# Attention's scores and row-max scores as pairs of matmuls in 64-column halves of TensorE

## The chip, the cores and the metric

The kernel runs on one core of a Trainium2 chip. Its time is the device time of one execution in microseconds (us), the median over several runs; the less the better. The engines are TensorE (PE in the rows; PEld is its weight load), VectorE (DVE), ScalarE (ACT), GpSimd (POOL) and SyncE (SP, which issues most DMAs). TensorE multiplies a stationary operand, the weights, of up to 128 rows (the contraction) and 128 columns (the partitions of the result) by a moving operand that is streamed through it, and writes to PSUM. Shapes in the rows are written 128\*64 (rows and columns of the weights) and 128x288 (partitions and streamed columns of the moving operand).

## What is computed

Three blocks follow each other. Attention over 4 batches of 8 heads, 1152 positions of 64 values, with the queries pooled by twos; then a router that sends each of 2304 tokens of 512 values to one of 8 experts; then a dense feed-forward block.

```python
def _attn_ref(q, k, v):
    B, H, S, D = q.shape                       # 4, 8, 1152, 64
    q_pool = q.reshape(B, H, S // 2, 2, D).mean(axis=3)
    scores = scale * np.matmul(q_pool, k.transpose(0, 1, 3, 2))
    scores = scores - np.max(scores, axis=-1, keepdims=True)
    attn = np.exp(scores)
    attn = attn / (np.sum(attn, axis=-1, keepdims=True) + 1e-09)
    return np.matmul(attn, v)
...
    logits = x @ w_gate + modality_bias[modality_id]      # router
    out[mask] = gate_w[mask, None] * (np.maximum(x[mask] @ w1[e], 0.0) @ w2[e])
...
    g = softplus(x @ w_in)                                # dense block
    return g @ w_out
```

## The kernel before

Attention is worked off by pairs of heads, 16 of them (`p`). For each pair there are float16 operands whose 128 rows hold the 64 values of a head twice: `KA` is the rounded key, in both halves; `Q[:,:,0]` holds the rounded query in one half and what the rounding left over in the other; `KB` and `Q[:,:,1]` hold the rest of the key against the rounded query, and in rows of the other half the row maximum that is subtracted. Every product of these contracts over all 128 rows.

Three steps on TensorE take nearly all of attention's time there:

- `srow` (L117, and L120 for the tile that holds 64 queries of each head): row-max scores of 128 queries against 384 keys into the tile `sr` (three buffers), 27 such rows a pair of heads. VectorE reduces each to its maximum (`mx`, L121). `mfin` turns the maxima of a pair into rows of `Q` (L140, L144).
- `smat` (L168, L169): the scores of 128 keys against 288 queries for both heads into `st` (two buffers), four matmuls; `ex` (L172, ScalarE) makes the exponentials `P` of them (five buffers). A pair of heads has 18 such groups (`g`), nine for each half of the queries.
- `pv` (L212): values times `P` in float32, the two heads in the two column halves of the array, 64 columns each, into `pv`.

Beside these, `add` (L186, POOL, L184 on DVE for one pair) sums `P` over three groups into `acc`, `rsum` (L197, L202) sums over partitions in 32-column matmuls, and after each batch of four pairs `lstage` does the router's steps for its tokens: sums and transposes (L227, L238, L285), ranks (L296 to L298), and a chain of small steps on VectorE.

The order is written by hand. For each group the main loop issues the scores of the next group, then its exponentials, then row-max rows (about 1.5 a group, some 27 groups ahead of need, by the formula in `rows`) between single steps of other work (casts of the next heads, loads, `rsum`, router steps), then `pv` for two groups at once at odd chunks and for one at the ninth, then `add`. Each engine works off its instructions in that order. On TensorE a group so reads: four scores in 128 columns, one or two row-max rows in 128 columns, and in about every second group four or eight pv matmuls in 64 columns.

After the 288th group come the router's last steps, the experts' blocks and the dense block; all their matmuls use float16 high and low parts.

Of the kernel before, what the change touches and what calls it, by code (L numbers as in the profile page):

```python
# [16 lines left out]
def attention(ctx,late,tc,I,C,x_dram,LG,gate,fill,early):  # L17

    nc=tc.nc
# [89 lines left out]
    def srow(r):  # L109
        p,w=divmod(r,SRN); t,kh=divmod(w,3)  # L110
        ka,q=KA[p%NS],Q[p%NS]
        if w==0: MX[p]=smp.tile([128,9,3],F32,name="mx")
        sr=srp.tile([128,512],F32,name="sr")
        h,r0=TILES[t]
        k0=kh*KW
        if h<2:
            nc.tensor.matmul(sr[:,:KW],lhsT=q[:,h,0,r0:r0+128],rhs=ka[:,h,k0:k0+KW],start=True,stop=True)  # L117
        else:
            for hh in range(2):
                nc.tensor.matmul(sr[64*hh:64*hh+64,:KW],lhsT=q[:,hh,0,r0:r0+64],rhs=ka[:,hh,k0:k0+KW],start=True,stop=True)  # L120
        nc.vector.tensor_reduce(out=MX[p][:,t,kh:kh+1],in_=sr[:,:KW],axis=AX.X,op=ALU.max,negate=True)  # L121

    def mfin(p,ta=0,tb=9):
# [36 lines left out]
    def dec(g):  # L160
        p,s=divmod(g,18); half,c=divmod(s,9)
        return p,half,c
    def smat(g):
        p,half,c=dec(g); ka,kb,q=KA[p%NS],KB[p%NS],Q[p%NS]
        st=stp.tile([128,2,512],F32,name="st"); ST[g]=st
        qs=slice(half*HQ,half*HQ+HQ); ks=slice(c*128,c*128+128)
        for h in range(2):
            nc.tensor.matmul(st[:,h,:HQ],lhsT=ka[:,h,ks],rhs=q[:,h,0,qs],start=True,stop=False)  # L168
            nc.tensor.matmul(st[:,h,:HQ],lhsT=kb[:,h,ks],rhs=q[:,h,1,qs],start=False,stop=True)  # L169
    def ex(g):  # L170
        P[g]=pp.tile([128,2,HQ],F32,name="P")
        nc.scalar.activation(out=P[g],in_=ST.pop(g)[:,:,:HQ],func=ACTF.Exp,scale=1.0/16)  # L172
# [235 lines left out]
    while done<6: srow(done); done+=1  # L408
    C['cl1'](); C['setup']()
    while done<15: srow(done); done+=1  # L410
# [4 lines left out]
    while done<R0: srow(done); done+=1  # L415
    for f in MF[1:]: f()
    smat(0); ex(0)
    ones()
    for g,f in C['later']: at(g,f)
# [7 lines left out]
    for g in range(NG+1):  # L427
        if g+1<NG: smat(g+1)
        if g>=1 and g-1<NG:
            p,half,c=dec(g-1)  # L430
            if c==NCH-1: evac(p,half)
        if g+1<NG: ex(g+1)
        tgt=rows(g)
        es=ev.pop(g,[])
        while pend and pend[0][0]<=g: pend.pop(0)[1]()
        while done<tgt-(g<18) or es:
            if done<tgt-(g<18): row(g)
            if es: es.pop(0)()

        if g<NG:  # L440
            c=dec(g)[2]
            for k in ((g-1,g) if c%2 else (g,) if c==NCH-1 else ()): pv(k)
        while done<tgt: row(g)
        if g<NG: add(g)
# [607 lines left out]
```

## Time and profile before

| | us |
|---|---|
| median of 3 runs | 1153.48 |
| lowest, highest of them | 1151.69, 1153.79 |
| profiled execution | 1149.53 |
| its span, first to last instruction | 1147.7 |
| attention's exponentials, first to last (L172) | 22.8 to 504 |

The profile is of one execution. Its rows give, for a group of instructions, line, engine, operation, the tile written and those read, the shapes and the count, then busy time and the mean duration in ns, then the time that the engine was idle just before. A matmul's duration goes from its start to the modelled end of its result, and following matmuls overlap; how fast TensorE works is therefore read from the starts. In a list in order of time, rows with a count hold several instructions of one kind, and their duration goes from the first start to the last end.

### The profile page before, as it was taken

The numbers are of one execution on the slowest core, as the hardware profiler recorded it, in microseconds if no ns is written. First come the engines' busy times: TensorE is split into PE (matmuls) and PEld (weight loads), VectorE is DVE, ScalarE is ACT, GpSimd is POOL, SyncE is SP. The second block draws the span as 40 slices with busy tenths as digits, with TensorE's granted clock in tenths as the row PEclk, the third lists the DMA queues.
The fourth block names the chain that finished last, engine by engine and source line by source line (L and its number), as shares of the span: only waits on it lengthen the run. The fifth ranks groups of instructions, "written<-read, shape, count | busy, mean of one in ns | idle before, by whom it ended". The sixth has DMA issues, their size and how long they took to land. (4 is left out here: it accounts for less than half of the span.)

```text
span 1147.7 us, 20868 instructions
## 1 busy us (share of the span) xinstructions
PE 1082.5 (94%) x7887; PEld 641.0 (56%) x7887; DVE 865.6 (75%) x1583; ACT 641.2 (56%) x1096; POOL 504.9 (44%) x532
## 2 busy tenths in 40 slices
PE   5998999999999999998989898999999999999996
PEld 2444555455555554566877777885444444446662
DVE  5778798768877787969789888739967767676762
ACT  5666656675666655556556556647444444444441
POOL 7888877888688867644423233110000100100101
PEclk9999999999999999999999999999999999999999
DMA  9334427441654041335677787731100000000000
GB/s 250 79 84 111 120 64 197 113 120 38 182 149 113 24 130 53 116 127 193 211 261 253 277 279 271 265 125 46 37 10 28 28 10 19 37 1 11 37 10 31
DMA packets 42940, 129.48 MB, mean 113 GB/s; under 512 B 5841, under 2 KB 12881, under 8 KB 40914
## 3 DMA queue, kind: packets, MB, share of 16 engines
q1 hardware_dynamic: 39794, 118.12, 34.2%
q0 software_dynamic: 3040, 9.96, 2.5%
q8 instruction: 65, 1.06, 0.4%
q14 instruction: 41, 0.34, 0.1%
HBM read 108.13 MB, written 20.45 MB: 112 GB/s over the span
## 5 line engine op out<-in xcount | busy, mean ns | idle before, releaser
L121 DVE TENSOR_REDUCE mx<-sr 128x1 f32<-128x384 f32 x432 | 225.4, 550 | 92.8 <-PE sr L117 73.9
L172 ACT ACTIVATE P<-st 128x576 f32<-128x576 f32 x288 | 186.0, 651 | 154.0 <-PE st L169 142.5
L186 POOL TENSOR_TENSOR acc<-P 128x288 f32<-128x288 f32 x192 | 160.6, 858 | 84.0 <-ACT P L172 80.3
L796 POOL DMA_INDIRECT out_dram<-io,CIDS x18 | 21.1, 1174 | 359.1 <-ACT io L794 312.7
L212 PE MATMUL pv<-P,v 128*64 128x288 f32 x1152 | 174.5, 419 | 0.3 <-ACT P L172 0.3
L168 PE MATMUL st<-Q,KA 128*128 128x288 f16 x576 | 155.4, 291 | 0.0
L169 PE MATMUL st<-Q,KB 128*128 128x288 f16 x576 | 153.6, 288 | 1.8 <-ACT Q L152 1.8
L186 POOL TENSOR_TENSOR acc<-acc,P 128x288 f32<-128x288 f32 x176 | 148.5, 864 | 9.0 <-ACT P L172 7.3
L117 PE MATMUL sr<-KA,Q 128*128 128x384 f16 x384 | 113.6, 335 | 17.2 <-DVE mx L121 8.7
L611 PE MATMUL l<-xf,WIH 128*128 128x256 f16 (+1 forms) x384 | 125.1, 326 | 1.0 <-ACT xf L817 1.0
L612 PE MATMUL l<-xf,WIH 128*128 128x256 f16 (+1 forms) x384 | 125.1, 326 | 0.2 <-DVE xf L818 0.2
L613 PE MATMUL l<-xf,wl 128*128 128x256 f16 (+1 forms) x384 | 125.1, 326 | 0.0
L648 ACT ACTIVATE mhl<-mraw 128x512 f16<-128x512 f32 x160 | 98.1, 625 | 45.3 <-DMA mraw<-in_wm_dram 22.2
L653 DVE SCALAR_TENSOR_TENSOR mhl<-mraw,mhl 128x512 f16<-128x512 f32 x140 | 95.7, 703 | 27.3 <-ACT mhl L648 26.5
L212 PEld LDWEIGHTS pv<-P,v 128*64 128x64 f32 x1152 | 70.4, 136 | 72.9 <-issue 35.6
L787 PE MATMUL o<-WOH,g 128*128 128x512 f16 x288 | 109.1, 379 | 1.2 <-ACT io L794 0.8
L788 PE MATMUL o<-wl,g 128*128 128x512 f16 x288 | 109.1, 379 | 0.0
L789 PE MATMUL o<-WOH,g 128*128 128x512 f16 x288 | 109.1, 379 | 0.0
L168 PEld LDWEIGHTS <-KA 128*128 128x128 f16 x576 | 56.3, 98 | 85.5 <-issue 75.4
L770 ACT ACTIVATE e<-e 128x1024 f32<-128x1024 f32 x36 | 38.0, 1057 | 101.3 <-DVE m L768 101.3
L94 POOL TENSOR_TENSOR KB<-kr,KA 64x576 f16<-64x576 f32 x64 | 83.3, 1305 | 4.3 <-ACT KA L90 2.1
L612 PE MATMUL l<-hT,mhl 128*128 128x256 f16 x288 | 78.5, 272 | 6.4 <-DVE hT L680 6.4
(246 smaller groups left out, 2162.0 us busy)
## 6 DMA issues: line engine op xcount, KB each, us to landing
mraw<-in_wm_dram SPq DMA_DIRECT2D x80, 512.0 KB
kr<-in_k_dram SPq DMA_DIRECT2D x30, 576.0 KB
qr<-in_q_dram SPq DMA_DIRECT2D x16, 576.0 KB
v<-in_v_dram SPq DMA_DIRECT2D x16, 576.0 KB
mraw<-in_w_out_dram SPq DMA_DIRECT2D x16, 512.0 KB
stg<-in_w_in_dram SPq DMA_DIRECT2D x12, 512.0 KB
y_dram<-w SPq DMA_DIRECT2D x20, 256.0 KB
xs_dram<-xs SPq DMA_DIRECT2D x24, 192.0 KB
```

Of the source, the lines that this page charges most:

```text
L117: nc.tensor.matmul(sr[:,:KW],lhsT=q[:,h,0,r0:r0+128],rhs=ka[:,h,k0:k0+KW],start=True,stop=True)
L121: nc.vector.tensor_reduce(out=MX[p][:,t,kh:kh+1],in_=sr[:,:KW],axis=AX.X,op=ALU.max,negate=True)
L168: nc.tensor.matmul(st[:,h,:HQ],lhsT=ka[:,h,ks],rhs=q[:,h,0,qs],start=True,stop=False)
L169: nc.tensor.matmul(st[:,h,:HQ],lhsT=kb[:,h,ks],rhs=q[:,h,1,qs],start=False,stop=True)
L172: nc.scalar.activation(out=P[g],in_=ST.pop(g)[:,:,:HQ],func=ACTF.Exp,scale=1.0/16)
L186: for h in range(2): nc.gpsimd.tensor_tensor(out=A[:,h],in0=B_[:,h],in1=P[g][:,h],op=ALU.add)
L212: nc.tensor.matmul(t[64*h:64*h+64,:HQ],lhsT=V[p][:,c,64*h:64*h+64],rhs=P[g][:,h],start=(c==0),stop=(c==NCH-1))
L611: nc.tensor.matmul(o,lhsT=wh_,rhs=x[0],start=first,stop=False)
L612: nc.tensor.matmul(o,lhsT=wh_,rhs=x[1],start=False,stop=False)
L613: nc.tensor.matmul(o,lhsT=wl_,rhs=x[0],start=False,stop=last)
L787: nc.tensor.matmul(o,lhsT=g[:,0,i,cs],rhs=WOH[:,fc],start=(fc==0),stop=False)
L788: nc.tensor.matmul(o,lhsT=g[:,0,i,cs],rhs=WOL(fc),start=False,stop=False)
```

## The change

Each matmul of the scores, 128 columns wide, becomes two of 64 columns: the first 64 keys into partitions 0 to 63 of `st`, the other 64 into partitions 64 to 127, with the same moving operand. Each row-max matmul of 128 columns becomes two of 64 queries in the same way, as those of L120 were already. The operands, their types and the sums are the same.

```diff
@@ srow
-        if h<2:
-            nc.tensor.matmul(sr[:,:KW],lhsT=q[:,h,0,r0:r0+128],rhs=ka[:,h,k0:k0+KW],start=True,stop=True)
-        else:
-            for hh in range(2):
-                nc.tensor.matmul(sr[64*hh:64*hh+64,:KW],lhsT=q[:,hh,0,r0:r0+64],rhs=ka[:,hh,k0:k0+KW],start=True,stop=True)
+        for i in range(2):
+            hh,r=(h,r0+64*i) if h<2 else (i,r0)
+            nc.tensor.matmul(sr[64*i:64*i+64,:KW],lhsT=q[:,hh,0,r:r+64],rhs=ka[:,hh,k0:k0+KW],start=True,stop=True)
@@ smat
-        qs=slice(half*HQ,half*HQ+HQ); ks=slice(c*128,c*128+128)
+        qs=slice(half*HQ,half*HQ+HQ)
         for h in range(2):
-            nc.tensor.matmul(st[:,h,:HQ],lhsT=ka[:,h,ks],rhs=q[:,h,0,qs],start=True,stop=False)
-            nc.tensor.matmul(st[:,h,:HQ],lhsT=kb[:,h,ks],rhs=q[:,h,1,qs],start=False,stop=True)
+            for i,w in enumerate((ka,kb)):
+                for o in (0,64):
+                    nc.tensor.matmul(st[o:o+64,h,:HQ],lhsT=w[:,h,c*128+o:c*128+o+64],rhs=q[:,h,i,qs],start=(i==0),stop=(i==1))
```

In the changed file the row-max matmuls stand in L118, the scores in L168, pv in L211, the transposes in L284 and the exponentials in L171. Two places show what it does to the order on TensorE. The first is the seam between row maxima, pv and the next scores; a row gives line, operation, result and operands, and the size of the result (the float32 matmuls of L212 load their weights themselves). Before:

```order
L169 LDWEIGHTS KB_194
L169 MATMUL st<-Q_197,KB_194 128x288
L117 LDWEIGHTS Q_196
L117 MATMUL sr<-KA_190,Q_196 128x384
L212 MATMUL pv<-P,v 64x288 x4
L168 LDWEIGHTS KA_191
L168 MATMUL st<-Q_197,KA_191 128x288
```

The same place now:

```order
L168 LDWEIGHTS KB_194
L168 MATMUL st<-Q_197,KB_194 64x288
L118 LDWEIGHTS Q_196
L118 MATMUL sr<-KA_190,Q_196 64x384
L118 LDWEIGHTS Q_196
L118 MATMUL sr<-KA_190,Q_196 64x384
L211 MATMUL pv<-P,v 64x288 x4
L168 LDWEIGHTS KA_191
L168 MATMUL st<-Q_197,KA_191 64x288
L168 LDWEIGHTS KA_191
L168 MATMUL st<-Q_197,KA_191 64x288
```

Where results of 128, 64 and 128 partitions followed each other, all have 64 now; nothing changes its place.

The second is a transpose of the router's stage (L285, `xu` against an identity, 96 columns, which are over 64). Before:

```order
L117 LDWEIGHTS Q_195
L117 MATMUL sr<-KA_189,Q_195 128x384
L285 MATMUL sr<-ident,xu 96x128 x4
L168 LDWEIGHTS KA_191
L168 MATMUL st<-Q_197,KA_191 128x288
```

And now:

```order
L118 LDWEIGHTS Q_195
L118 MATMUL sr<-KA_189,Q_195 64x384
L118 LDWEIGHTS Q_195
L118 MATMUL sr<-KA_189,Q_195 64x384
L284 MATMUL sr<-ident,xu 96x128 x4
L168 LDWEIGHTS KA_191
L168 MATMUL st<-Q_197,KA_191 64x288
```

Here the transposes, which stood among wide matmuls, stand between 64-column ones. Counted over the whole program, steps between the wide and the 64-column form are 358 before and 74 now, steps to or from 32-column matmuls 110 in both.

## Rows read from the trace of the kernel before

**Rows 1.** The page, part 1: engine, busy us, share of span, instructions.

```profile
PE 1082.5 (94%) x7887; PEld 641.0 (56%) x7887; DVE 865.6 (75%) x1583; ACT 641.2 (56%) x1096; POOL 504.9 (44%) x532
```

**Rows 2.** Four stretches: length, busy us (instructions) by engine, granted clock, DMA.

```profile
core 0: us, PE busy (x) PEld busy (x) DVE busy (x) ACT busy (x) POOL busy (x), PEclk, DMA share, GB/s
181.56:301.86 120.30, 117.48 (x946) 61.40 (x944) 93.95 (x206) 78.05 (x142) 99.36 (x113) 1.00 0.44 118
211.09:224.56 13.47, 13.47 (x105) 7.05 (x103) 11.73 (x19) 10.50 (x19) 11.91 (x13) 1.00 0.78 215
239.74:253.21 13.47, 13.47 (x105) 7.05 (x103) 11.04 (x21) 10.51 (x19) 12.72 (x13) 1.00 0.86 242
268.44:284.87 16.43, 15.34 (x131) 8.29 (x131) 16.09 (x41) 10.98 (x22) 14.74 (x16) 1.00 0.17 53
```

**Rows 3.** Waits from 60 to 490 us: total us, times, longest us.

```profile
ACT P L172 <- PE st L169: 125.5, 137, 3.6
POOL acc L186 <- ACT P L172: 80.6, 66, 3.1
...
DVE mx L121 <- PE sr L117: 60.9, 77, 2.1
...
ACT P L172 <- POOL acc L186: 8.7, 18, 1.1
...
PE sr L117 <- DVE mx L121: 6.4, 7, 2.1
```

**Rows 4.** Groups of TensorE's instructions by line and shape, the whole span.

```profile
L212 PE MATMUL pv<-P,v 128*64 128x288 f32 x1152 | 174.5, 419 | 0.3 <-ACT P L172 0.3
L168 PE MATMUL st<-Q,KA 128*128 128x288 f16 x576 | 155.4, 291 | 0.0
L169 PE MATMUL st<-Q,KB 128*128 128x288 f16 x576 | 153.6, 288 | 1.8 <-ACT Q L152 1.8
L117 PE MATMUL sr<-KA,Q 128*128 128x384 f16 x384 | 113.6, 335 | 17.2 <-DVE mx L121 8.7 <-ACT KA L90 8.2
...
L120 PE MATMUL sr<-KA,Q 128*64 128x384 f16 x96 | 16.8, 356 | 2.7 <-DVE Q L86 1.4 <-DVE mx L121 0.8
```

**Rows 5.** TensorE's matmuls in order of time, 300 to 304 us: start, duration.

```profile
300.03 1.14 PE L212 MATMUL pv<-P,v 128*64 128x288 f32 x8
301.10 0.30 PE L168 MATMUL st<-Q,KA 128*128 128x288 f16 x1
...
301.48 0.29 PE L169 MATMUL st<-Q,KB 128*128 128x288 f16 x1
301.69 0.35 PE L120 MATMUL sr<-KA,Q 128*64 128x384 f16 x2
301.98 0.64 PE L285 MATMUL sr<-ident,xu 128*96 128x128 f32 x4
302.45 0.33 PE L117 MATMUL sr<-KA,Q 128*128 128x384 f16 x1
302.71 0.71 PE L212 MATMUL pv<-P,v 128*64 128x288 f32 x4
303.35 0.30 PE L168 MATMUL st<-Q,KA 128*128 128x288 f16 x1
...
303.85 0.33 PE L117 MATMUL sr<-KA,Q 128*128 128x384 f16 x1
304.01 0.38 PE L285 MATMUL sr<-ident,xu 128*96 128x128 f32 x2
```

**Rows 6.** Matmuls and weight loads in order of time, 58.5 to 59.4 us.

```profile
58.75 0.14 PEld L120 LDWEIGHTS <-Q 128*64 128x64 f16 x4 [0.24 <-issue]
58.75 0.52 PE L120 MATMUL sr<-KA,Q 128*64 128x384 f16 x4
...
58.94 0.55 PEld L212 LDWEIGHTS pv<-P,v 128*64 128x64 f32 x6
...
59.10 0.65 PE L212 MATMUL pv<-P,v 128*64 128x288 f32 x4
```

## The prediction, made before the changed kernel was run

> **What bounds the kernel now.** I read the busy times of the page first, then the stretches of the attention loop, then who waits for whom, and last the starts of single matmuls. TensorE (PE) is busy for 94% of the span, VectorE (DVE) for 75%, GpSimd (POOL) for 44% [rows 1]. The change touches only attention, so its stretches count. Four pairs of heads (72 groups) repeat there every 120.30 us, at a granted clock of 1.00; in that period PE is busy 117.5 us, POOL 99.4, DVE 94.0 and ACT 78.1 [rows 2]. The list of waits has the same direction everywhere: from 60 to 490 us the exponentials on ACT wait 125.5 us for the score matmuls, POOL 80.6 us for the exponentials, the row maxima on DVE 60.9 us for the row-max matmuls, while the row-max matmuls wait only 6.4 us for a buffer that DVE frees, and ACT 8.7 us for a buffer that POOL frees [rows 3]. PE sets the pace; DVE and POOL are each some 80% loaded and wait for it.
>
> Busy PE is not PE at its peak, so the starts of the matmuls have to be read. Wide matmuls of 288 columns follow each other every 0.125 us: the four scores from 303.35 take until the L117 at 303.85 [rows 5]. The pv matmuls (L212) run as pairs in two column halves. Two pairs last 0.65 us where nothing is in their way (59.10, [rows 6]), four last 1.14 (300.03, [rows 5]): 0.49 us for two more, so a pair every 0.245 us, and 0.405 us from a matmul's start to its end. Now the seams. The last of the four pairs starts at 300.76 (300.03 and three times 0.245) and the next wide matmul at 301.10, 0.34 us instead of 0.245: **leaving the 64-column form costs 0.10 us.** From the wide L117 at 302.45 to L212 it is 0.26 us; from the same kind of L117 at 303.85 to the wide L285 it is 0.16: 0.10 us on entering. Then the two pairs from 302.71 last 0.71 instead of 0.65 us: another 0.05 to 0.06, because its weights were not loaded ahead. **Entering pv costs 0.15 us.** From L169 at 301.48 to the row-max pair L120 it is 0.21 instead of 0.125, 0.09, and such a first pair takes 0.19 us until the next one (58.75 to 58.94) where the second takes 0.16 (58.94 to 59.10) [rows 6]: together 0.11. It is not the change of type: L117 (float16) to L285 (float32) at 303.85 shows no loss, and neither does L120 (float16) to L212 (float32) from 58.94 to 59.10 [rows 5, 6].
>
> **The change, part by part.** It takes no arithmetic out. Each of 1152 wide score matmuls (L168 and as many of L169) becomes a pair, and so do the 384 wide row-max matmuls; the 96 narrow row-max matmuls and the 1152 of pv are narrow already [rows 4]. PE gets 1536 more matmuls and as many more weight loads; the order of the work is the same on every engine but for a few rows on ACT near 500 us, which I cost at nothing: a copy and an exponential trade places while ACT waits for PE.
>
> What goes are seams. In the order of the instructions 329 steps between the wide and the 64-column form go: 127 into pv, 33 into narrow row-max pairs, 169 back into wide matmuls. New are 45, around what stays wide (transposes, ranks, the early expert blocks). Those that lead to 32-column matmuls stay, with another neighbour. The sum of PE time: 127 x 0.15 = 19.0, 33 x 0.11 = 3.6, 169 x 0.10 = 16.9, together 39.5 us; a new seam at 0.12 us (301.69 to 301.98, from a row-max pair to a transpose, is 0.29 where 0.16 would do [rows 5]; with what DVE's waits at the rank matmuls hide I leave it there), 45 x 0.12 = 5.4 us. **Net 34 us on PE, 284 seams of 0.12 us.**
>
> What the pairs themselves cost is not in the trace for scores: no float16 pair of 288 columns runs there. The near rows bound it. From below: a pv pair of 288 float32 columns takes 0.245 us, just twice the 0.125 of one wide float16 matmul, and the second row-max pair at 58.94 takes 0.16 us, as a wide one does; so a pair that has its weights takes as long as the wide matmul, and no gain is possible in it, the columns being streamed as before. From above: the first pair after a seam takes 0.03 us more, with its loads uncovered. The loads are covered where the pairs follow each other: four loads of two row-max pairs are done in 0.14 us, and the loads of pv start at 58.94, in the moment in which the last row-max pair starts [rows 6]. I take nothing for it; at 0.03 us the 1536 pairs would take back 46 us.
>
> The Trainium skill has a rule against this: "TensorEngine Tiling (Array Packing)", section Restrictions and Gotchas, says that column tiling excludes the Fast Weight Load, and "TensorE: Matmul & The Clock Gate", Part 3, that a load overlaps matmuls in flight only where the row groups differ or where it goes to the background weight buffer. All pairs here use all 128 rows. The loads at 58.94 run beside matmuls on the same rows, so the trace speaks for the second half of that sentence; by its first half alone the third rival below would be the forecast.
>
> **How much of the 34 us arrives.** PE is the pace, but not by far. The period of 120.30 us has 82 seams less and 12 more: 70 x 0.12 = 8.4 us, so 111.9, in which POOL's 99.4 us would be 89% and DVE's 94.0 84% [rows 2]. Stretch by stretch it is tighter. The nine groups from 211.09 lose 10 seams, 13.47 to 12.27 us, with DVE busy 11.73: it fits, barely, and I take 1.0 of 1.2. Those from 239.74 also lose 10, but POOL has 12.72 us of work there: at most 0.75, I take 0.7. Those from 268.44, with the router's steps on DVE, lose a net 3, 16.43 to 16.07, and DVE has 16.09: I take 0.2 of 0.36 [rows 2]. So 1.9 of 2.76 in these three, the tightest of their kinds, and nearly all elsewhere: about three quarters. Queues smooth it: five P buffers let POOL lag some four groups, three sr buffers let DVE lag three row maxima. What is late next is then POOL's acc for the P buffers (the wait of 8.7 us grows) and DVE's mx for the sr buffers (the 6.4 us). Of the 34 us, 30 seams (3.6 us) lie before 60 us, where loading and DVE hold PE too: half. The other 30.5 at three quarters are 23: **25 us in all.** After attention nothing is changed, and what is there starts after its end, so that the gain is carried to the end. The profiled execution took 1149.53 us: 1124.5. The median of the three runs is 4 us above it, 1153.48: **1128.5 us.**
>
> **Rivals.**
> 1. DVE and POOL take the pace over, because they need their slack within three to six groups and not nine: the stretches from 239.74 and 268.44 are then the rule. Against it: both wait for PE for most of their idle time [rows 3]. Gain 10 to 19 us, say 14.5: 1139.
> 2. Everything arrives, since a DVE or POOL burst in one stretch is made good in the next: 34 us, 1119.5. For it: utilisation in the period stays under 90%.
> 3. **Slower:** the weight loads of float16 pairs are not covered. One mechanism, at every pair of the scores, where only 0.125 us lie between one pair's start and the next, in which two loads have to end; it decides from 34/1536 = 22 ns a pair on. At 0.03 to 0.05 us (the first pairs after a seam, [rows 5, 6]) it costs 46 to 77 us: some 1153.5-34+60 = 1180. Against it: the loads at 58.75, four in 0.14 us [rows 6].
> 4. The change does not do what it says: the 0.10 us belong to pv's end and not to the form, and stay in front of the narrow scores. For it: no row shows a narrow float16 matmul behind pv. Against it: the same 0.09 to 0.10 us stand on entering, in front of L120 as in front of L212. The entering half alone goes then, 22.6 of the 39.5 us, less 5.4 for the new seams 17, of which some 10 arrive past DVE and POOL: 1143; if neither half goes, 1153.
>
> **How the numbers follow.** Forecast 0.60 (own range 1121 to 1134), rival 1 0.19, rival 2 0.09, rival 3 0.06, rival 4 0.06, half of it at no change. The range takes in the forecast, rival 2 and nearly all of rival 1: 1118 to 1141. A measurement of this kernel tells about 0.2% (2.3 us) from no change. Faster by more: 0.60+0.19+0.09+0.03 = 0.91; same 0.03; slower 0.06.
>
> **What would show it.** Right: a score pair starts 0.24 us after the last pv pair, not 0.34; score pairs follow each other every 0.125 us, with their loads starting beside the pair before; the period of 120.3 us falls to 112 to 115 us; DVE and POOL keep their busy time and their share rises; after attention all is alike but earlier. Wrong: score pairs every 0.15 us or more (rival 3), 0.34 us still behind pv (rival 4), or the seams gone and the matmuls waiting for mx or P in their place (rival 1).

## The result, and the profile after

| | before | after |
|---|---|---|
| median of 9 runs each, us | 1152.55 | 1139.08 |
| lowest, highest, us | 1147.16, 1154.40 | 1133.89, 1145.03 |
| profiled execution, its span, us | 1149.53, 1147.7 | 1137.12, 1135.3 |
| attention's exponentials, first to last, us | 22.8 to 503.6 | 22.7 to 488.0 |

The ratio is 0.9884, with an interval of 0.9864 to 0.9904: 13.5 us faster. The forecast of 25 us was right in its sign and about twice the size; the time lies where the first rival put it, 1139.

The page's first part, after; engine, busy us, share, instructions [rows 1]:

```profile
PE 1058.7 (93%) x9423; PEld 707.6 (62%) x9423; DVE 870.0 (77%) x1583; ACT 640.8 (56%) x1096; POOL 502.3 (44%) x532
```

PE has 1536 more matmuls and is busy 23.8 us less. But its idle time, span less busy, rose from 65.2 to 76.6 us. DVE and POOL kept their busy time, within 4.4 and 2.6 us, as expected.

In attention alone, from the first exponential to the last, PE's busy time fell by 27.0 us, though two stretches at half clock there (below) lengthen it by up to 3.4. First the kernel before, then the changed one:

```profile
core 0: us, PE busy (x) PEld busy (x) DVE busy (x) ACT busy (x) POOL busy (x), PEclk, DMA share, GB/s
22.80:503.60 480.80, 463.52 (x3696) 241.46 (x3695) 380.08 (x808) 305.27 (x554) 385.16 (x431) 1.00 0.40 109
22.70:488.00 465.30, 436.49 (x5213) 306.48 (x5210) 384.08 (x804) 305.75 (x555) 382.17 (x431) 0.99 0.41 113
```

The seam of [rows 5] in the timeline of PE, after (start, duration):

```profile
290.23 1.14 PE L211 MATMUL pv<-P,v 128*64 128x288 f32 x8
291.20 0.29 PE L168 MATMUL st<-Q,KA 128*64 128x288 f16 x2
291.32 0.29 PE L168 MATMUL st<-Q,KB 128*64 128x288 f16 x2
291.44 0.29 PE L168 MATMUL st<-Q,KA 128*64 128x288 f16 x2
291.56 0.29 PE L168 MATMUL st<-Q,KB 128*64 128x288 f16 x2
291.69 0.33 PE L118 MATMUL sr<-KA,Q 128*64 128x384 f16 x2
```

The last of the four pv pairs starts at 290.23 and three times 0.245, 290.965; the first score pair comes 0.235 us later, where it was 0.34. From there a pair starts every 0.12 us, as fast as one wide matmul did. The weight loads are hidden; a load and a matmul pair a little earlier:

```profile
288.65 0.29 PE L168 MATMUL st<-Q,KA 128*64 128x288 f16 x2
288.65 0.12 PEld L168 LDWEIGHTS <-KB 128*64 128x64 f16 x2
```

While the `KA` pair of 288.65 streams, the two `KB` loads of the pair that follows at 288.78 take 0.12 us: they just fit. A new seam, from a row-max pair to a transpose, costs 0.10 us over the 0.16 between two row-max pairs:

```profile
292.34 0.33 PE L118 MATMUL sr<-KA,Q 128*64 128x384 f16 x2
...
292.60 0.31 PE L284 MATMUL sr<-ident,xu 128*96 128x128 f32 x1
```

So the prices read at single places hold. What differs is what became of the sum, stretch by stretch. The table has the time of 18 groups (one pair of heads, from its first exponential to the next pair's), and the gain on PE worked out with the prediction's prices from the seams in the order of that pair, all in us; the sixteen pairs' gains add up to 34.0.

| pair of heads | seams' worth | before | after | gained |
|---|---|---|---|---|
| 5 (as 9) | 2.44 | 29.53 | 27.18 | 2.35 |
| 6 (as 10) | 2.60 | 28.65 | 26.77 | 1.88 |
| 7 (as 11) | 2.24 | 28.70 | 27.14 | 1.56 |
| 1 | 2.56 | 30.43 | 32.20 | -1.77 |
| 4, with router steps | 1.16 | 33.44 | 33.09 | 0.35 |
| 8, with router steps | 1.16 | 33.42 | 36.22 | -2.80 |
| 12, with router steps | 1.16 | 33.41 | 34.01 | -0.60 |
| 13 | 2.03 | 31.60 | 31.11 | 0.49 |
| all 16, from the first to the last exponential | 34.0 | 480.8 | 465.3 | 15.5 |

The plain pairs of the middle got 70 to 96% of their worth. The three router pairs together lost 3.0 us where the seams were worth 3.5, and pair 1 lost 1.8 where it should have won 2.6. These four alone miss 10.9 of the 18.5 us that did not arrive in attention. The stretches of [rows 2], after: the period of four pairs, the nine groups with 13.47 us before and the nine groups after them with DMA, the nine with router steps; then pair 12 and pair 1.

```profile
177.77:295.08 117.31, 111.72 (x1331) 78.58 (x1329) 94.55 (x206) 78.40 (x142) 98.72 (x113) 0.99 0.44 121
204.95:218.00 13.05, 12.55 (x158) 9.49 (x156) 11.49 (x19) 10.61 (x19) 11.62 (x13) 1.00 0.81 222
231.72:244.51 12.79, 12.66 (x158) 9.43 (x156) 11.22 (x21) 10.50 (x18) 12.63 (x14) 1.00 0.87 246
258.86:277.49 18.63, 16.18 (x177) 10.12 (x173) 15.88 (x41) 11.17 (x22) 14.12 (x17) 0.91 0.17 47
376.19:410.20 34.01, 29.94 (x358) 19.50 (x354) 32.07 (x88) 20.17 (x38) 25.92 (x31) 1.00 0.34 89
54.84:87.04 32.20, 27.86 (x322) 19.27 (x324) 22.91 (x41) 19.37 (x35) 26.22 (x30) 0.95 0.30 76
```

The same two pairs of before:

```profile
388.74:422.15 33.41, 31.30 (x265) 16.93 (x264) 30.92 (x87) 19.94 (x39) 26.16 (x30) 1.00 0.33 90
56.16:86.59 30.43, 28.51 (x222) 14.62 (x224) 20.99 (x41) 19.40 (x35) 26.21 (x31) 1.00 0.32 80
```

In pair 12 PE's busy time fell by 1.36 us, more than the 1.16 worked out, and the pair is 0.60 longer: PE is idle 4.07 us in it instead of 2.11. The period has 117.31 us where 112 to 115 was expected. PEclk is below 1 in the rows of the period, of the router's nine groups and of pair 1, which no stretch of [rows 2] showed. Three stretches run at 0.50, that is at 1.2 instead of 2.4 GHz:

```profile
74.90:78.30 3.40, 3.40 (x31) 1.72 (x28) 0.84 (x2) 0.71 (x2) 3.24 (x4) 0.50 0.09 21
266.10:269.50 3.40, 3.40 (x24) 2.11 (x24) 2.16 (x8) 1.32 (x2) 1.07 (x2) 0.50 0.02 5
692.70:696.10 3.40, 3.40 (x18) 2.65 (x17) 2.65 (x6) 1.00 (x2) 0.00 (x0) 0.50 1.04 404
```

Each follows waits of PE. Before the first it is one long wait, before the second there are two in the router's chain (timeline of PE, what it waited for in brackets), and before the third two of 0.94 and 0.99 us in the expert blocks:

```profile
70.13 0.36 PE L118 MATMUL sr<-KA,Q 128*64 128x384 f16 x2
73.84 0.35 PE L118 MATMUL sr<-KA,Q 128*64 128x384 f16 x2 [3.36 <-DVE mx L119]
...
263.81 0.69 PE L196 MATMUL sr<-acc,one 128*32 128x288 f32 x8 [1.48 <-DVE f L261]
...
265.91 0.17 PE L295 MATMUL sr<-OH,tri 96*96 96x8 f16 x1 [0.97 <-DVE OH L265]
```

What a fall goes with can be read off pairs 8 and 12, which hold the same instructions: 36.22 us with one, 34.01 without, 2.2 us. In 3.40 us at half clock PE does at most 1.7 us of work less, so the rest of the 2.2 is something else. The profile of before has no such stretch before its last few us, but that execution was a lucky one: its mean granted clock is 0.998, where the other runs of that kernel have 0.991 to 0.998 and those of the changed kernel 0.986 to 0.993 (0.993 the profiled one). So the kernel before has such stretches too, only fewer. The medians of all runs, 0.996 and 0.990, are 0.006 apart; as an estimate from them, that is at most 6.8 of 1139 us.

The list of waits from 60 to 490 us, after, against [rows 3]:

```profile
PE sr L118 <- DVE mx L119: 13.2, 14, 3.4
...
ACT P L171 <- POOL acc L185: 10.0, 14, 1.7
...
PE sr L295 <- DVE OH L265: 3.2, 5, 1.0
...
PE sr L196 <- DVE f L261: 3.0, 2, 1.5
```

PE's wait for the row maxima doubled, from 6.4 to 13.2 us; ACT's wait for POOL grew only from 8.7 to 10.0. PE's waits for the router's steps on DVE stand in the list of before as well, which [rows 3] does not show:

```profile
PE sr L296 <- DVE mx L121: 3.0, 3, 1.0
...
PE sr L296 <- DVE OH L266: 1.5, 3, 0.5
```

### The profile page after: what moved, and what is told of

Same layout as the page of the kernel before. It is cut to its first block, busy times and chain, and to the rows that moved or that the text cites. A ratio compares the mean times of both kernels' runs of the same rounds, so it can differ in the third digit from the quotient of the medians.

```text
span 1135.3 us, 23941 instructions
## 1 busy us (share of the span) xinstructions
PE 1058.7 (93%) x9423; PEld 707.6 (62%) x9423; DVE 870.0 (77%) x1583; ACT 640.8 (56%) x1096; POOL 502.3 (44%) x532
## 5 line engine op out<-in xcount | busy, mean ns | idle before, releaser
L171 ACT ACTIVATE P<-st 128x576 f32<-128x576 f32 x288 | 185.9, 650 | 132.9 <-PE st L168 120.1
L211 PE MATMUL pv<-P,v 128*64 128x288 f32 x1152 | 171.4, 411 | 0.5 <-ACT P L171 0.5
L118 PE MATMUL sr<-KA,Q 128*64 128x384 f16 x864 | 137.1, 340 | 26.7 <-DVE mx L119 16.2
L168 PE MATMUL st<-Q,KB 128*64 128x288 f16 x1152 | 159.2, 289 | 1.6 <-ACT Q L150 1.6
L168 PE MATMUL st<-Q,KA 128*64 128x288 f16 x1152 | 159.9, 290 | 0.0
L211 PEld LDWEIGHTS pv<-P,v 128*64 128x64 f32 x1152 | 86.0, 138 | 30.7 <-ACT P L171 3.5
L118 PEld LDWEIGHTS <-Q 128*64 128x64 f16 x864 | 58.3, 111 | 53.0 <-issue 37.0
L168 PEld LDWEIGHTS <-KB 128*64 128x64 f16 x1152 | 73.3, 111 | 24.4 <-issue 2.3
L168 PEld LDWEIGHTS <-KA 128*64 128x64 f16 x1152 | 73.2, 111 | 22.8 <-issue 6.0
```

The costliest lines, as they stand in the source:

```text
L118: nc.tensor.matmul(sr[64*i:64*i+64,:KW],lhsT=q[:,hh,0,r:r+64],rhs=ka[:,hh,k0:k0+KW],start=True,stop=True)
L168: nc.tensor.matmul(st[o:o+64,h,:HQ],lhsT=w[:,h,c*128+o:c*128+o+64],rhs=q[:,h,i,qs],start=(i==0),stop=(i==1))
L211: nc.tensor.matmul(t[64*h:64*h+64,:HQ],lhsT=V[p][:,c,64*h:64*h+64],rhs=P[g][:,h],start=(c==0),stop=(c==NCH-1))
```

## The experiments

Two theories stood against each other after the result. **A:** the seams gave their 34 us on PE, and what did not arrive is DVE's lateness (with POOL, which slows it). **B:** the pairs themselves cost something that eats the gain, or fewer seams went than counted. The ratios below are each to the kernel before in the same session, whose median there stands beside it. Kernel 3 is the kernel of experiment 3, and so on.

**1. Scores as pairs, row maxima wide.** This puts the row maxima of the changed kernel back:

```diff
-        for i in range(2):
-            hh,r=(h,r0+64*i) if h<2 else (i,r0)
-            nc.tensor.matmul(sr[64*i:64*i+64,:KW],lhsT=q[:,hh,0,r:r+64], ...
+        if h<2:
+            nc.tensor.matmul(sr[:,:KW],lhsT=q[:,h,0,r0:r0+128], ...
+        else:
+            ...
```

> The scores alone as pairs, the row maxima wide as before. Theory (the seams between the wide and the 64-column form are what costs, a pair itself costs nothing): steps between the two forms rise from 358 to 498, 140 more at 0.11 to 0.12 us, so some 15 us SLOWER than before, about 1168 us. Rival (the pairs themselves are faster or slower than wide matmuls, by a share of what was measured for both parts together, -13.5 us): scores are 1152 of the 1536 pairs, so about 10 us faster, 1142 us.

**2. Row maxima as pairs, scores wide.** The other half of the change:

```diff
-            for i,w in enumerate((ka,kb)):
-                for o in (0,64):
-                    nc.tensor.matmul(st[o:o+64,h,:HQ],lhsT=w[:,h,c*128+o:c*128+o+64], ...
+            nc.tensor.matmul(st[:,h,:HQ],lhsT=ka[:,h,ks],rhs=q[:,h,0,qs],start=True,stop=False)
+            nc.tensor.matmul(st[:,h,:HQ],lhsT=kb[:,h,ks],rhs=q[:,h,1,qs],start=False,stop=True)
```

> The row maxima alone as pairs, the scores wide as before. Theory (seams): 560 steps between the forms, 202 more than before, at 0.11 to 0.12 us some 22 to 24 us SLOWER than before, about 1175 us, and slower than with the scores alone. Rival (pairs): a quarter of the 13.5 us, 3 us faster, 1149 us.

Measured (before 1154.87): 1159.84 us for the scores alone, 1.0056 [1.0032, 1.0081]; 1163.43 us for the row maxima alone, 1.0087 [1.0056, 1.0118]. **Each half of the change alone makes the kernel slower, and both together faster.** In the order the steps between the wide and the 64-column form are 358 before, 498 with the scores alone, 560 with the row maxima alone, 74 with both. No price of a pair can do that, so theory B falls, and the fourth rival with it. The price is read in attention alone (after it the two profiles have 10.2 and 3.4 us at half clock before their last few us, and that of before none). The scores alone ahead:

```profile
23.20:509.30 486.10, 476.96 (x4843) 261.10 (x4840) 376.43 (x804) 307.25 (x555) 379.90 (x430) 1.00 0.40 108
22.80:514.50 491.70, 481.31 (x4067) 239.03 (x4065) 376.90 (x808) 307.19 (x554) 381.77 (x431) 1.00 0.40 107
```

Against the 463.52 us of before PE is busy 13.4 us more for 140 seams, 0.096 each, and 17.8 us more for 202, 0.088 each. That is at the lower end of what was read at single seams, 0.09 to 0.15. The seam can be seen where it now is, between a score pair and a wide row-max matmul, 0.23 us where 0.12 to 0.125 would do, and it is gone behind pv (the two pv pairs last 0.71 us instead of 0.65, so the second starts some 0.305 us after 290.59, and the scores follow 0.22 us later); timeline of PE with the scores alone:

```profile
290.59 0.71 PE L213 MATMUL pv<-P,v 128*64 128x288 f32 x4
291.12 0.29 PE L170 MATMUL st<-Q,KA 128*64 128x288 f16 x2
...
291.49 0.29 PE L170 MATMUL st<-Q,KB 128*64 128x288 f16 x2
291.72 0.34 PE L117 MATMUL sr<-KA,Q 128*128 128x384 f16 x1
```

The times rose by 5.0 and 8.6 us, less than PE's work, and the expectations were two to three times too high. In the wait list of the second kernel PE's wait for `mx` is 3.5 us where before had 6.4 [rows 3]: a slower PE finds DVE done.

**3 and 4. A lighter DVE.** The row-max reduce takes half of its columns, on the kernel before and on the changed one. Both leave out half of the row maximum.

```diff
-        nc.vector.tensor_reduce(out=MX[p][:,t,kh:kh+1],in_=sr[:,:KW], ...
+        nc.vector.tensor_reduce(out=MX[p][:,t,kh:kh+1],in_=sr[:,:KW//2], ...
```

> The kernel before, with VectorE's row maxima taken over 192 of the 384 columns (the maximum is so taken over half of the keys; the matmuls are all there). It frees some 0.2 us on VectorE for each of 432 rows. Both theories: TensorE paces, only its waits of 22 us in attention shrink: 5 to 12 us faster than before, 1141 to 1148 us.

> The changed kernel, with VectorE's row maxima taken over 192 of the 384 columns, as in the run beside it. Theory (the missing 20 us went to waits for VectorE, mainly in the pairs of heads with the router's steps, and the clock's falls follow these waits): against the kernel before with the same lighter VectorE it gains 28 to 34 us, about 1112 us, and no fall of the granted clock is seen in attention. Rival 1 (GpSimd or ScalarE took the gain): against its partner still 12 to 18 us, about 1130 us. Rival 2 (the clock falls by itself, whether or not TensorE waits): the falls stay and the gain is 20 to 25 us.

Measured (before 1154.87): 1149.12 us, 0.9958 [0.9937, 0.9978], for the kernel before; 1117.06 us, 0.9692 [0.9658, 0.9726], for the changed one. Between the two lie 32.1 us. PE's busy time, from the pages of the two in this order, differs by 33.1 us:

```profile
PE 1081.3 (94%) x7887; PEld 641.1 (56%) x7887; DVE 784.2 (68%) x1583; ACT 640.0 (56%) x1096; POOL 500.4 (44%) x532
```

```profile
PE 1048.2 (94%) x9423; PEld 700.1 (63%) x9423; DVE 791.2 (71%) x1583; ACT 641.7 (58%) x1096; POOL 507.2 (46%) x532
```

That is near the 34, but two things come together in it. Outside the router pairs 4, 8 and 12 attention got 26.1 us shorter (371.6 to 345.5), of 30.5 worked out; without the lighter DVE it was 18.6 (380.6 to 361.9). **So a lighter DVE brings 7.5 of the 11.9 us that were missing there.** The router pairs do not gain by it: the three take 99.3 us in kernel 4, 100.3 in the kernel before. They add 6.5 us to the difference only because kernel 3 has them longer than the kernel before, 105.8 us in all, in pair 12 with a stretch at half clock:

```profile
385.52:421.77 36.25, 32.98 (x265) 17.54 (x264) 29.77 (x87) 19.92 (x38) 25.55 (x30) 0.95 0.33 85
```

Why the lighter DVE lengthened them stays open. So the medians, 5.8 us from the relief before the change and 22 after it (0.9884 to 0.9692 of about 1153), overstate the contrast; outside the router pairs it is 9.0 against 16.5. POOL's work is unchanged, so POOL alone does not hold the time. Pair 12 of the changed kernel takes 33.48 us with the lighter DVE, where it took 34.01:

```profile
360.21:393.69 33.48, 30.16 (x358) 19.73 (x354) 28.89 (x87) 20.08 (x39) 25.78 (x31) 1.00 0.34 93
```

DVE's busy time in it fell from 32.07 to 28.89 us and the pair hardly moved: it is not the sum of DVE's work that sets it.

**5 to 8. Two ways to take load from DVE, which failed.** One moves the sums and remainders of `Q` for three more pairs of heads (6, 10, 14) from DVE to POOL; the other draws more row-max rows out of the router's stretches (`DV` is the number of rows by which they run ahead where a router stretch begins); then both; then the first on the kernel before.

```diff
-        ...; ve=nc.gpsimd if p==1 else nc.vector
+        ...; ve=nc.gpsimd if p in (1,6,10,14) else nc.vector
```

> The changed kernel; the three casts of the queries (one sum, two remainders) of the pairs of heads 6, 10 and 14, which fall into the router's stretches, run on GpSimd instead of VectorE. VectorE gets 3.3 us less to do in each of the three stretches where it is busy 31 to 32 of 33 to 36 us. Theory (in these stretches the gain was lost to VectorE): each becomes 1.5 to 3 us shorter, 4 to 8 us in all, 1131 to 1135 us. Rival (GpSimd, or the clock by itself, holds these stretches): no gain, or a loss through GpSimd, 1138 to 1143 us.

```diff
-    DV=4.5; FL=-0.6
+    DV=6.5; FL=-0.6
```

> The changed kernel; the row maxima run further ahead before each router stretch (the constant DV at 6.5 instead of 4.5), so that 14 instead of 18 rows fall into it and 1.6 to 2.2 us of VectorE's work move to stretches with room. Theory: 1 to 2 us from each of three stretches, 1133 to 1137 us. Rival (VectorE's load there is not what holds): 1139 us.

> Both edits together on the changed kernel. Theory: VectorE has 5 us less to do in each router stretch and TensorE paces there again: 6 to 11 us, 1128 to 1133 us; not the full sum of the two, as TensorE then bounds. Rival: 1139 us.

> The kernel before with the casts of pairs 6, 10 and 14 on GpSimd. Theory (before the change these stretches wait some 3 us each for VectorE, much of it in the router's own chain): 0 to 3 us faster than before, less than the same edit brings to the changed kernel. Rival (the edit helps by itself, with the change or without): the same gain as on the changed kernel.

Measured (before 1150.75): casts on POOL 1163.91, 1.0115 [1.0081, 1.0149]; `DV` of 6.5 1177.29, 1.0235 [1.0201, 1.0268]; both 1189.08, 1.0348 [1.0305, 1.0390]; casts on POOL before the change 1181.19, 1.0262 [1.0215, 1.0309]. All four expectations missed in sign. The casts do the same harm without the change, so they say nothing against theory A; they show how POOL works on DVE. In the timeline of DVE with the casts on POOL, three operations of 8 elements take 5.71 us and three of 17 take 2.67:

```profile
159.19 5.71 DVE L279 TENSOR_SCALAR r<-r,gate 96x8 f32<-96x8 f32 x3
...
164.82 2.67 DVE L306 TENSOR_SCALAR cm<-cc,RK 96x17 f32<-96x17 f32 x3
```

In that time POOL works without a gap. The third of the three, the POOL operations in its time, and then what PE waited for:

```profile
161.07 3.83 DVE L279 TENSOR_SCALAR r<-r,gate 96x8 f32<-96x8 f32 x1
...
161.84 1.54 POOL L185 TENSOR_TENSOR acc<-P 128x288 f32<-128x288 f32 x2
163.33 1.54 POOL L185 TENSOR_TENSOR acc<-acc,P 128x288 f32<-128x288 f32 x2
...
168.09 1.09 PE L284 MATMUL sr<-ident,xu 128*96 128x128 f32 x4 [6.52 <-DVE mx L119]
```

In the changed kernel, where POOL pauses, the same operations take 0.22 us each. Here the three of L279 take 1.20, 0.84 and 3.83, and each ends 0.03 us after the end of a POOL operation, the last one after five of them. **DVE's small steps stand behind POOL's operations, one or several in a row.** The Trainium skill, "SBUF — State Buffer", section Who interferes with whom, says that a VectorE instruction with two SBUF inputs contends with a GpSimd instruction that reads SBUF, through a port pair that one of them holds for a whole instruction. The ends in these rows agree with a hold for whole instructions. Whether a TENSOR_SCALAR, with one tensor and a scalar for each partition, falls under that sentence was not tried apart; the casts of experiment 12, which have two inputs in SBUF, do. Behind these waits the clock falls too (mean granted clock 0.984), so the loss is not DVE's waits alone.

With `DV` at 6.5 PE waits longer for the row maxima; the wait list has

```profile
PE sr L118 <- DVE mx L119: 27.1, 28, 4.4
```

twice the 13.2 of the changed kernel, and the mean granted clock is 0.978. What made DVE late there was not followed further.

**9 and 10. Fewer small steps on DVE.** Four steps of the router, written as three TENSOR_SCALARs for three tiles of tokens, become one TENSOR_TENSOR with the scalar broadcast, as the last stage had them already; on the changed kernel, then on the one before.

```diff
-            if last: V.tensor_tensor(out=T('d',[96,3,8]),in0=lg,in1=e3(z['m']),op=ALU.subtract)
+            if 1: V.tensor_tensor(out=T('d',[96,3,8]),in0=lg,in1=e3(z['m']),op=ALU.subtract)
...
```

> The changed kernel; in the router's stretches four steps on VectorE that are written as three operations each (d, OH, r, cm; 24 operations and 8.2 us in the 34.0 us of the pair of heads from 376.19) are one operation each, as in the router's last step. No wait is moved, no work leaves VectorE otherwise. At 0.17 to 0.35 us an operation VectorE has 5.5 to 7 us less to do in each of three stretches. Theory (VectorE's load in these stretches takes the gain back): each becomes 2 to 4 us shorter, 6 to 12 us in all, 1127 to 1133 us. Rival (the gain is lost elsewhere, or to the clock by itself): within 2 us of the changed kernel.

> The kernel before with the same four steps as one operation each. Theory: TensorE paces there, but waits some 3 to 4 us in each of these stretches for VectorE: 3 to 8 us faster than before, less than the edit brings to the changed kernel, so that the distance between the two grows from 13.5 to 16 to 22 us. Rival (VectorE is not what took the gain): the same gain in both, a distance of 13.5 us.

Measured (before 1151.95): 1127.38 us, 0.9761 [0.9719, 0.9804], on the changed kernel; 1148.35 us, 0.9965 [0.9933, 0.9996], on the one before. **The same edit is worth 3.6 us before the change and 14 after it** (0.9884 to 0.9761; by the intervals 0.5 to 8 and 9 to 20), and the change is worth 21 us with it, 13.5 without. In the profiles the three router pairs got 3.6 us shorter before the change and 8.1 after it, about 2 of these by the stretch at half clock in pair 8, which is gone. Pair 12 in the changed kernel with merged steps:

```profile
369.74:401.77 32.03, 30.08 (x358) 19.51 (x354) 29.71 (x72) 19.85 (x38) 26.42 (x31) 1.00 0.35 94
```

and in the kernel before with merged steps:

```profile
386.82:419.01 32.19, 31.14 (x265) 16.79 (x264) 29.20 (x71) 19.94 (x39) 26.09 (x30) 1.00 0.36 93
```

Against 34.01 and 33.41 that is 2.0 and 1.2 us, for 16 DVE instructions less. DVE's busy time fell to 29.71 us, less far than with the halved reduces of kernel 4, and the pair got shorter by more. The loss of the router pairs is gone. Pair 4 now has 1.13 us of its 1.16 (32.28 to 31.15); in pairs 8 and 12 (32.20 to 32.04, 32.19 to 32.03) nearly nothing of it shows.

**11. Rows drawn back.** `DV` at 3.0 on kernel 9, since the router's stretches had room now:

```diff
-    DV=4.5; FL=-0.6
+    DV=3.0; FL=-0.6
```

> As e9_after_merged, with the row maxima spread more evenly (DV at 3.0 instead of 4.5): 3 rows more fall into each router stretch, now that VectorE has room there, and 3 fewer into the pairs before it. Theory: a further 0 to 4 us, since fewer rows run against inputs that are not cast yet: 1124 to 1131 us. Rival (the lead of 4.5 still fits): up to 4 us slower than e9_after_merged.

Measured (before 1151.95): 1138.84 us, 0.9850 [0.9801, 0.9898], 11.5 us slower than kernel 9, beyond the rival's 4. Of the three leads tried 4.5 is the best (6.5 was tried on the changed kernel, 3.0 on kernel 9).

**12. One collision.** In pair 1 a remainder of `Q` on DVE (L86) meets two remainders of the key on POOL (L94). DVE's row and POOL's row in the changed kernel:

```profile
69.92 3.40 DVE L86 TENSOR_TENSOR Q<-qs,Q 64x576 f16<-64x576 f32 x1
...
69.45 2.51 POOL L94 TENSOR_TENSOR KB<-kr,KA 64x576 f16<-64x576 f32 x2
```

and before:

```profile
72.28 1.42 DVE L86 TENSOR_TENSOR Q<-qs,Q 64x576 f16<-64x576 f32 x1
...
71.81 3.02 POOL L94 TENSOR_TENSOR KB<-kr,KA 64x576 f16<-64x576 f32 x2
```

DVE's one operation takes 3.40 us instead of 1.42, the row maxima queue behind it, and PE waits the 3.36 us at 73.84 that were shown above. It starts 0.47 us after POOL's first remainder in both kernels (69.92 and 69.45, 72.28 and 71.81), so the two do not overlap in another way. Before, it got through after one POOL operation, which ended at 73.08, and POOL's second took 1.79 us instead of 1.27; in the changed kernel it got through only after three, the last of which ended at 72.71. Every profile that has this meeting has the same 0.47 us; it takes 1.42 us in the kernels before or with one half of the change, 3.40 in those with both halves. What decides it was not found. On kernel 9 POOL's four remainders of that pair come a few steps later:

```diff
-                (7,cq(0,1)),(9,cq(1,1)),(6,ckl(0,0)),(7,ckl(0,1)),(9,ckl(1,0)),(11,ckl(1,1))]
+                (7,cq(0,1)),(9,cq(1,1))]+[(k,ckl(j//2,j%2)) for j,k in enumerate((10,11,12,14) if p==3 else (6,7,9,11))]
```

> As e9_after_merged, with the four casts of the keys' remainders of the fourth pair of heads (L94, GpSimd) 3 to 4 groups later; VectorE's order is the same. In the changed kernel a cast on VectorE (L86) takes 3.40 us at 69.92, while GpSimd works on two of these casts until 71.96, where it takes 1.42 us before; TensorE waits 3.4 us for it and its granted clock falls at 74.9 us. Theory (the long cast is VectorE standing behind GpSimd's casts, and the clock falls because TensorE waited): the cast takes 1.3 to 2 us, the wait is under 1.7 us, no fall near 75 us, and the kernel is 2 to 5 us faster than e9_after_merged, 1122 to 1125 us. Rival (another cause, the cast stays at 3.4 us, or the next collision follows some groups later): within 1.5 us of e9_after_merged, 1126 to 1129 us.

Measured (before 1159.90): 1122.55 us, 0.9722 [0.9650, 0.9795]. The ratio's interval overlaps that of kernel 9; the profile is clear where the edit acts: attention is 3.95 us shorter than in kernel 9, 3.9 of it in pair 1. DVE's row, and pair 1:

```profile
70.43 0.75 DVE L86 TENSOR_TENSOR Q<-qs,Q 64x576 f16<-64x576 f32 x1
```

```profile
55.34:83.34 28.00, 26.30 (x322) 18.71 (x324) 20.35 (x41) 19.37 (x36) 24.28 (x29) 1.00 0.35 87
```

The cast takes 0.75 us, the pair 28.00 instead of 31.91 in kernel 9, and the granted clock is 1.00 in it. That is 2.43 us less than the 30.43 of before, of a worth of 2.56. By its median **kernel 12 is the fastest that computes the reference**, 2.8% under the kernel before.

## Why the prediction was half right

**The seams: right.** 0.10 us on leaving pv, 0.10 on entering a wide matmul, pairs as fast as wide matmuls. In attention PE's busy time is 31.3 us less in kernel 12 than in kernel 10, the same edit without the change (463.20 to 431.95 us, neither with a stretch at half clock there): 0.11 for each of the 284 seams, of 0.12 forecast. The two half changes bear out the count from the other side, at 0.09 to 0.10. The third rival was wrong: two loads in 0.12 us fit beside a pair of 288 columns, though only just.

**"How much of the 34 us arrives": wrong.** Three quarters was taken; it was 15.5 us at attention's end and 13.5 in the medians. The measured 1139.08 lies outside the forecast's own 1121 to 1134; it is in the stated range only because that takes in most of the first rival. The three quarters do not follow from the stretches either: 1.9 of 2.76 us there and nearly all of the other 5.6 would be some 7.5 of the period's 8.4, nine tenths. That the lower share was written brought the forecast nearer by luck; the period gained 3.0 us (120.30 to 117.31). The term that failed is the stretches' share. The nine groups from 211.09 gave 0.42 us where 1.0 was taken (13.47 to 13.05), those from 239.74 the 0.7 that was taken (13.47 to 12.79), and those from 268.44 lost 2.2 where 0.2 was taken (16.43 to 18.63). In it lie three things:

1. *The router's stretches.* I compared DVE's 16.09 us of work with 16.07 of PE's and gave the stretch 0.2 us of gain. It lost instead: pairs 4, 8 and 12 together were 3.0 us longer. A sum of busy time is the wrong measure there, since these steps are a chain: PE's sums and ranks wait for DVE's `f` and `OH` (1.48 and 0.97 us in the rows above), and DVE's next steps for them. Halving the reduces took 3.2 us of DVE's work out of pair 12 and left it at 33.48; fewer steps in the chain took out 2.4 and brought it to 32.03. PE's waits at the rank matmuls were in the list of before, 3.0 and 1.5 us, and I left them out of the rows.
2. *A collision of DVE and POOL in pair 1.* One DVE operation took 3.40 us instead of 1.42, behind three POOL operations instead of one. Kernel 12 shows that this cost the pair its gain; why the same meeting came out otherwise stays open. I had used POOL's 89% only as POOL's own limit. POOL was not late (ACT's wait for it grew by 1.3 us); it made DVE late.
3. *The clock.* I held it at 1.00. Three stretches of the profile are at 0.50, each behind waits of PE and each at most 1.7 us of PE's work. Where the wait of pair 1 went, in kernel 12, the stretch at half clock behind it went too.

**"After attention all is alike but earlier": wrong in one place.** The lead of 15.5 us is there until 689 us of the profile after and is 12.6 at 710; the stretch at half clock from 692.70 lies between. Why the clock fell there, behind waits of 0.94 and 0.99 us in the expert blocks that use none of the changed code, was not settled. Such falls come and go: the profile of kernel 10 has them after attention also, at 528.6 and 579.8 us, and that of kernel 3 has one in attention, at 410.4.

**The first rival** had the time, 1139, and the releaser, DVE. Its reason, slack needed within a few groups, is near the mark for the router's stretches; its second place, POOL's tight nine groups from 239.74, is not: they gained the 0.7 that the forecast took. **The second rival**, everything arrives, comes near outside the router pairs where DVE is lighter: 26.1 of 30.5 us in kernel 4.

**What stays open.** Kernels 9 and 12 bring back 16.5 us against the changed kernel, but merged steps help the kernel before as well, by 3.6. With them the change is worth 21 us, and by the profile of pair 1 some 4 more with the collision gone (whether the kernel before gains from that edit was not run). From kernel 10 to kernel 12 attention gets 24.0 us shorter (476.6 to 452.6), so 10 of the 34 us are not accounted for by an edit: 2.0 in the router pairs 8 and 12, 1.5 in pair 13 (31.11 us in the changed kernel, 31.12 in kernels 9 and 12), 3.0 in the six plain pairs of the middle, and the rest in the first and the last pairs. Some 3 us of the 10 PE's busy time did not lose either (31.3 of 34).

## What to carry to other kernels

Read the form of TensorE's matmuls along its queue. A step between 128- and 64-column tiles cost 0.09 to 0.12 us here, and splitting a wide matmul into a 64-column pair cost nothing at 288 streamed columns; so this queue gained when all were put into one form, and lost when only some were. Before counting such a gain, look for the stretches where another engine's chain returns to TensorE, and test them by making that engine lighter, on the kernel before and on the changed one, pair by pair: a difference of two such kernels can look full because one of them got worse in another place. A chain is shortened by fewer steps, not by less work beside it. And when the pace-setting engine gets faster, look at the operations of the other two that run at the same time, VectorE's and GpSimd's above all: their starts alone did not tell here which waits for which.

## What was not expected of the hardware

- DVE's small operations with a scalar for each partition took from 0.22 to 3.83 us, and a cast of 64x576 took 0.75, 1.42 or 3.40 us: alone, behind one POOL operation, or behind three, though it started 0.47 us after POOL's first in both of the last two cases.
- The granted clock fell to 0.50 three times in the profile of a kernel whose PE is busy 93% of the time, each time behind waits of PE of about one to three us. The runs of the kernel before show it too, but less: mean granted clock 0.991 to 0.998 against 0.986 to 0.993.
